# Four small moves on VectorE and its port in an attention plus two-MLP kernel: decoding units on ScalarE, one-input forms, the port in the plan, half the planning cushion

## Chip, core and metric

The kernel runs on one core of a Trainium2 chip. The metric is device time in microseconds (us), of which the median over several runs is compared. The engines are named as in the profile: PE is the matrix engine (PEld its weight loads), DVE is VectorE, ACT is ScalarE, POOL is GpSimd, SP is the queue that issues most of the DMAs.

## What is computed

Causal attention with a decay bias, then a SoLU MLP with a norm, then a second MLP, on 4 batches of 576 tokens (2304 rows) with 8 heads of 64:

```
scores = q @ k.T / 8, masked causally, + min(bias, 0)
bias   = -(cum[row] - cum[col]),  cum = cumsum(max(s, 0))
attn   = exp(scores - rowmax) / (rowsum + 1e-9);   x = attn @ v
h  = x @ w_in (512 x 1024);  e = softmax(h);  y = h * e
ln = (y - mean(y)) / sqrt(var(y) + 1e-6) * g_ln;   x2 = ln @ w_out (1024 x 512)
h2 = x2 @ w2_in (512 x 2048);  g = h2 * clip(h2 + 3, 0, 6) / 6;  out = g @ w2_out (2048 x 512)
```

The weights of the MLPs come as 64-bit floats, so each has to be decoded on the chip. Every matrix that enters a product is split into a high and a low part in the matmul's reduced 32-bit format, and a product is three matmuls (high by high, high by low, low by high).

## The kernel before

**Order.** Nothing is ordered by hand. Every operation is put on a list (`plan.add`) with its engine, a planned duration, the things that it reads and writes and the buffers that it takes. `Plan.emit` then plays the list through: at each step the engine that can start first takes the ready operation of the lowest rank, its planned duration is added, and the order in which the operations start in this play is the order in which they are written out. On the chip every engine runs its own queue in that order. The durations thus set only the order, and never a time on the chip. Two more things enter the play: an operation with `port=True` (all of POOL's unless told otherwise, and some of DVE's) starts only once the last one with the port has ended, and `plan.spare`, set when the first attention round has been listed, adds a cushion to each later operation of an engine.

**Stages.** Four attention rounds, one for each batch, then what is left of the first MLP, then the second. In round one the heads go in pairs: scores on PE, then `tops` (DVE: adds the mask, takes the row minimum of the negated scores, frees the PSUM bank), `both` (DVE: joins the minima of a row cut in two), `exp` (ACT), `inv` (DVE: reciprocal of the row sum) and `go` (POOL: scales the rows), then transposes on PE, copies out of PSUM on DVE and ACT, and the product with V. Beside it run the decoding of the first MLP's weights and its first tiles. In the rounds behind it PE works on the scores of one batch and the first MLP's tiles of the batch before, with an early part of the second MLP's weights in the background.

**Decoding.** `split64` takes 512 columns of 64-bit words for each of 128 rows: a load (`raw_wi` for `w_in`, `raw_wo` for `w_out`, 8 blocks each, issued from ACT's queue), `high` on ACT (the upper word, L369), `units` on DVE (three bits of the lower word, made an integer 0 to 7, L373, tile `t_wi` or `t_wo`), `join` on DVE (shift and or, L377, tile `a_wi` or `a_wo`), `put_hi` (ACT, or DVE for the first four blocks, L384), and `put_lo` (POOL for `w_in`, L393; DVE for `w_out`, L391). The tiles `a` and `t` have one buffer each, so that a block's `high` waits until the block before has gone through `put_lo`, and its `units` until the `join` before has read `t`. The second MLP's weights go through `decoded` in the same way, with its own `units` on DVE.

Of the kernel before, what the change touches and what calls it, by code (L numbers as in the profile page):

```python
# [10 lines left out]
F32 = mybir.dt.float32  # L11
F32R = mybir.dt.float32r
I32 = mybir.dt.int32
U32 = mybir.dt.uint32
BF16 = mybir.dt.bfloat16
AF = mybir.ActivationFunctionType
ALU = mybir.AluOpType
# [22 lines left out]
HI_IN = 4  # L40
# [139 lines left out]
def dve2(n):  # L180
    return 0.11 + 0.00053 * n
# [15 lines left out]
def kernel(ctx, tc, q, k, v, s, w_in, w_out, g_ln, w2_in, w2_out, out):  # L197
    nc = tc.nc
# [4 lines left out]
    P = 128  # L203
# [9 lines left out]
    NQ = len(SZ)  # L213
# [4 lines left out]
    const = ctx.enter_context(tc.tile_pool(name="const", bufs=1))  # L218
# [3 lines left out]
    sums = const.tile([P, NH, NQ], F32, name="sums")  # L222
    rsum = const.tile([P, NH, NQ], F32, name="rsum")
    nmax = const.tile([P, NH, NQ + 1], F32, name="nmax")
    halfs = const.tile([P, 1], F32, name="halfs")
# [21 lines left out]
    def w_out_at(x, c):  # L247
        late = c >= KFF - LATE_OUT
        return w_out_t[x, late][:, c - (KFF - LATE_OUT) * late, :]
# [95 lines left out]

    def split64(plan, pool, src, hi, lo, name, key, scale=None, bufs=1, ring="", raws64=2, after=(), hi_dve=False, on_dve=(), on_pool=(), behind=None, needs=(), home=()):

# [23 lines left out]
        def units():  # L371
            T["t"] = pool_at().tile([P, n], I32, tag="dec_e", name=f"t_{name}", bufs=bufs)
            (nc.gpsimd if "units" in on_pool else nc.vector).tensor_scalar(T["t"], T["raw"][:, :, 0].bitcast(U32), 2.0**-29, 7.0, ALU.mult, ALU.min)  # L373

# [13 lines left out]
        def put_lo():  # L388
# [10 lines left out]
            lambda: plan.add("ACT", 0.61, high, reads=[w], writes=[a], new=[("dec_a" + ring, bufs, a)]),  # L399
            lambda: plan.add(*(("POOL", 0.85) if "units" in on_pool else ("DVE", 0.6)), units, reads=[w], writes=[t], new=[("dec_e" + ring, bufs, t)]),  # L400
            lambda: plan.add("DVE", 0.64, join, reads=[t], writes=[a]),
            lambda: plan.add(*(("DVE", 0.42) if hi_dve else ("ACT", 0.62 if scale is None else 0.71)), put_hi, reads=[a, *home], writes=[f"{key}/h{name}"]),
            lambda: plan.add(*(("DVE", 0.72) if scale is not None or "low" in on_dve else ("POOL", 1.4)), put_lo, reads=[a, f"{key}/h{name}"], writes=[f"{key}/l{name}"]),
        ]
# [10 lines left out]
    def decoded(pool_at, x, k, tags, ready):  # L415
# [6 lines left out]
        def block(o):  # L422
# [22 lines left out]
            for f in (  # L445
                lambda: plan.add("SP", 1.5, load, reads=[ready] if ready else [], writes=[raw], new=[(raw_tag, 1, raw)], lag=2.0),
                lambda: plan.add("ACT", 0.61, high, reads=[raw], writes=[f"{a_key}/{o}"], new=[(a_tag, 1, a_key)] if o == 0 else []),
                lambda: plan.add("DVE", 0.45, units, reads=[raw], writes=[t], new=[(t_tag, 1, t)]),
                lambda: plan.add("DVE", 0.65, join, reads=[t], writes=[f"{a_key}/{o}"], port=True),
            ):  # L450
                f()
# [68 lines left out]
    def load_w_in(c):  # L520
        f = slice((c // KDM) * 512, (c // KDM) * 512 + 512)
        c %= KDM
        done.append([f"win/hwi{c}_{f.start // 512}"])
        return split64(plan, dec, w_in[c * P : (c + 1) * P, f], w_in_h[:, c, f], w_in_l[:, c, f], f"wi{c}_{f.start // 512}", "win", after=["HL0k/h0"], behind=done[-3], hi_dve=c + f.start // 128 < HI_IN)

    def load_w_out(c):
        late = c >= KFF - LATE_OUT
        key = "wlate" if late else "wout"
        done.append([f"{key}/hwo{c}"])
        first = [lambda: plan.add("ACT", 0.0, lambda: w_out_part(True), writes=["wlate/"], new=[("wlate", 1, "wlate")])] if c == KFF - LATE_OUT else []  # L530
        return first + split64(plan, dec, w_out[c * P : (c + 1) * P, :], lambda: w_out_at("h", c), lambda: w_out_at("l", c), f"wo{c}", key, g_sb[:, c : c + 1], behind=done[-3])

# [194 lines left out]
    def exps(h, t, pieces):  # L727
        n, w = SZ[t], ST[t] + SZ[t]

        def both():  # L730
            nc.vector.tensor_tensor(nmax[:n, h, t : t + 1], nmax[:n, h, t : t + 1], nmax[:n, h, NQ : NQ + 1], ALU.min)

# [103 lines left out]
    def norm_part(heads, part):  # L836
# [4 lines left out]
        def inv():  # L841
            r = rsum[:, h0 : h1 + 1, ts[0] : ts[-1] + 1]
            nc.vector.tensor_scalar_add(r, sums[:, h0 : h1 + 1, ts[0] : ts[-1] + 1], 1.0e-9)
            nc.vector.reciprocal(r, r)
# [138 lines left out]
    def ffn1_x(i):  # L983
# [18 lines left out]
        x_keys = [f"x{b}/{hp}_{a}" for _, n, b, o in spans for hp in range(NPAIR) for a in range(2) if (o < CUT if a == 0 else o + n > CUT)]  # L1002
        plan.add("DVE", dve2(512), high, reads=x_keys, writes=[f"xs{i}/h"], new=[("xs", 2, f"xs{i}")])
        plan.add("POOL", pool_tt(512), low, reads=x_keys + [f"xs{i}/h"], writes=[f"xs{i}/l"])
# [15 lines left out]
    def ffn1_stats(i):  # L1020
# [6 lines left out]
        def both():  # L1027
            nc.vector.tensor_tensor(st(2), st(0), st(1), ALU.min)

# [164 lines left out]
    for b, share in enumerate(SHARES):  # L1194
        main = []
        if b == 0:
# [5 lines left out]
            mix(main, mixed([x[:2] for x in first_tiles], early[len(early) // 4 :]))  # L1202
            plan.spare = {"DVE": 0.06, "ACT": 0.1, "POOL": 0}
            continue
# [441 lines left out]
```

## Time and profile before

| | |
|---|---|
| three runs | 806.32, 810.79, 811.64 us, median 810.79 |
| the profiled execution | 803.45 us, of which its span is 801.6 us |
| PE busy | 769.8 us, 96% of the span |
| DVE busy | 606.9 us, 76% |
| ACT busy | 470.9 us, 59% |
| POOL busy | 230.1 us, 29% |

Busy time is the time in which an engine has at least one instruction of its own under way. An instruction that has been taken up and waits for something inside the engine counts as busy. The chain is the work that ended last, followed back from the end of the span to what released each step. All times of the trace are counted from the start of the span.

### The profile page before, as it was taken

To read this page: it belongs to the slowest core of one execution; us is meant where nothing else is said; L and a number is where in the kernel's file an instruction comes from. 1 tells how busy PE (TensorE), PEld (TensorE's weight loads), DVE (VectorE), ACT (ScalarE), POOL (GpSimd) and SP (SyncE) were. 2 spreads that over 40 slices of the span, in tenths; PEclk is the share of its full clock that TensorE was granted. 3 is DMA by queue.
4 is the path that set the end of the run, shared out by engine and by line. 5 is a ranking of instruction groups with operands and counts; after the bars stand their busy time and mean duration, and the time that the engine had idled before them with its cause. 6 is when DMAs were issued, how large, how long until landed. Compare 5 with 4: busy or idle time off the path is not lost.

```text
span 801.6 us, 15887 instructions
## 1 busy us (share of the span) xinstructions
PE 769.8 (96%) x5560; PEld 705.3 (88%) x5560; DVE 606.9 (76%) x1389; ACT 470.9 (59%) x1055; POOL 230.1 (29%) x320
## 2 busy tenths in 40 slices
PE   6779999999999999999999999999997999999998
PEld 5556777988897989888999999999997999999997
DVE  6989977877867688645879898988886876666662
ACT  4758867856765667655474766666674444444441
POOL 3566454334631636343300000000122002222221
PEclk9989999999999999999999999999999999999999
DMA  9947478868668857614151755667499654444440
GB/s 211 209 117 204 112 198 195 211 188 221 147 169 203 230 138 190 181 28 145 37 188 56 246 168 172 203 204 261 142 292 372 214 142 129 129 130 132 132 130 27
DMA packets 157616, 136.34 MB, mean 170 GB/s; under 512 B 67616, under 2 KB 135200, under 8 KB 157536
## 3 DMA queue, kind: packets, MB, share of 16 engines
q1 hardware_dynamic: 153600, 122.07, 54.4%
q10 hardware_dynamic: 2400, 8.54, 3.3%
q0 software_dynamic: 1536, 4.72, 1.6%
q8 instruction: 44, 0.72, 0.4%
q14 instruction: 36, 0.29, 0.1%
HBM read 74.67 MB, written 39.39 MB: 142 GB/s over the span
## 4 chain that ended last, share of the span: by engine, by line
PE 85%; DVE 7%; DMA 4%; ACT 1%; issue 1%; POOL 1%; SPq 0%; DVEq 0%; ACTq 0%
PE bank L1531 22%; PE bank L1354 21%; PE bank L1104 12%; PE bank L1014 11%; PE bank L909 6%; PE bank L814 5%; PE bank L882 5%; PE bank L1083 2%; DVE y L723 1%; PE bank L663 1%; DMA stage<-wt_d 1%; DVE t_wi L373 1%; PE bank L778 1%; POOL y L848 1%; DMA s_sb<-in_s_dram 1%
## 5 line engine op out<-in xcount | busy, mean ns | idle before, releaser
L1354 PE MATMUL bank<-xb,ws 128*128 128x384 f32 x1008 | 176.9, 335 | 3.7 <-ACT c L1367 3.4
L1354 PEld LDWEIGHTS bank<-xb,ws 128*128 128x128 f32 x1008 | 174.4, 188 | 4.7 <-ACT c L1367 4.1
L1531 PE MATMUL bank<-W,fs 128*128 128x256 f32 x864 | 106.8, 283 | 0.3 <-ACT c L1540 0.3
L1531 PEld LDWEIGHTS bank<-W,fs 128*128 128x128 f32 x864 | 105.0, 192 | 0.5 <-ACT c L1540 0.5
L830 POOL TENSOR_SCALAR y<-y,rsum 128x128 f32<-128x128 f32 (+4 forms) x120 | 72.1, 619 | 96.6 <-DVE rsum L826 59.2
L723 DVE CUSTOM_DVE_ANT_0 y<-bank,mask 96x288 f32<-96x288 f32 (+4 forms) x168 | 74.1, 465 | 26.8 <-PE bank L814 23.6
L735 ACT ACTIVATE y<-y,nmax 128x128 f32<-128x128 f32 (+4 forms) x140 | 83.4, 597 | 16.4 <-DVE nmax L723 12.9
L1104 PE MATMUL bank<-zh,w_out_h 128*128 128x256 f32 x288 | 83.5, 290 | 0.7 <-DVE zl L1090 0.7
L1531 PE MATMUL bank<-W,fa 128*128 128x256 f32 x648 | 81.5, 283 | 2.4 <-ACT fa L1508 1.9
L1531 PEld LDWEIGHTS bank<-W,fa 128*128 128x128 f32 x648 | 79.4, 192 | 2.8 <-ACT fa L1508 2.1
L1104 PE MATMUL bank<-zl,w_out_h 128*128 128x256 f32 x288 | 81.0, 281 | 0.1
L1104 PE MATMUL bank<-zh,w_out_l 128*128 128x256 f32 x288 | 80.9, 281 | 0.0
L1388 POOL DMA_DIRECT2D g_d<-g x24 | 13.1, 549 | 187.7 <-DVE g L1383 187.7
L814 PE MATMUL bank<-stack 128*96 128x288 f32 (+4 forms) x288 | 58.4, 319 | 3.2 <-DMA stack<-rows_d 1.7
L1014 PE MATMUL bank<-w_in_h,xh 128*128 128x512 f32 x144 | 60.3, 419 | 0.0
L882 PE MATMUL bank<-ident,y 128*128 128x128 f32 (+2 forms) x420 | 52.2, 261 | 6.1 <-DVE nmax L723 3.6
L1104 PEld LDWEIGHTS bank<-zh,w_out_h 128*128 128x128 f32 x288 | 54.2, 188 | 2.9 <-DVE zl L1090 1.1
L1014 PE MATMUL bank<-w_in_h,xl 128*128 128x512 f32 x144 | 56.6, 393 | 0.0
L1014 PE MATMUL bank<-w_in_l,xh 128*128 128x512 f32 x144 | 56.5, 392 | 0.0
L1508 ACT CAST fs<-r 128x1024 fp32r<-128x1024 f32 x27 | 28.3, 1048 | 45.4 <-PE bank L1531 23.6
L1104 PEld LDWEIGHTS bank<-zh,w_out_l 128*128 128x128 f32 x288 | 54.3, 189 | 0.4
L1104 PEld LDWEIGHTS bank<-zl,w_out_h 128*128 128x128 f32 x288 | 54.3, 188 | 0.3 <-DVE zl L1090 0.3
(274 smaller groups left out, 1576.0 us busy)
## 6 DMA issues: line engine op xcount, KB each, us to landing
r<-g_d SPq DMA_DIRECT2D x36, 512.0 KB
g_d<-g SPq DMA_DIRECT2D x72, 192.0 KB
rawo<-in_moe_w_out_dram SPq DMA_DIRECT2D x16, 512.0 KB
rawi<-in_moe_w_in_dram SPq DMA_DIRECT2D x16, 512.0 KB
x_d<-x2s SPq DMA_DIRECT2D x36, 128.0 KB
xr<-x_d SPq DMA_DIRECT2D x6, 768.0 KB
g_d<-g POOLq DMA_DIRECT2D x24, 192.0 KB, 5.4
W<-wp_d SPq DMA_DIRECT2D x6, 768.0 KB
```

The lines of the kernel that those rows point to most:

```text
L723: nc.vector.tensor_tensor_reduce(out=ys[h, t][:n, c0:c1], in0=bank(key)[:n, : c1 - c0], in1=mask[:n, 480 + n - w + c0 : 480 + n - w + c1], ...
L735: nc.scalar.activation(out=y[:n], in_=y[:n], func=AF.Exp, bias=nmax[:n, h, t : t + 1], scale=-1.0, accum_out=sums[:n, h, t : t + 1])
L814: nc.tensor.matmul(bank(key)[:n, : c1 - c0], lhsT=ss[:, 2 - 2 * m, ST[t] : w], rhs=ss[:, 3 - 2 * m, c0:c1], start=(m == 0), stop=(m == 1))
L830: nc.gpsimd.tensor_scalar(ys[h, t][:n], ys[h, t][:n], rsum[:n, h, t : t + 1], 1.0, ALU.mult, ALU.mult)
L882: nc.tensor.transpose(bank(key)[: SZ[jj], c : c + SZ[t]], ys[h, t][: SZ[t], ST[jj] : ST[jj] + SZ[jj]], ident[: SZ[t], : SZ[t]])
L909: nc.tensor.matmul(bank(key)[j * D : (j + 1) * D, lo - c0 : c1 - c0], lhsT=vs[v_key(p, a)][:n, jj, j, :], rhs=pts[pt_key(2 * p + j, a)][:n ...
L1014: nc.tensor.matmul(bank(key), lhsT=xs[i][m // 2][:, kk, :], rhs=(w_in_l if m == 1 else w_in_h)[:, kk, f * 512 : (f + 1) * 512], start=(kk ...
L1083: nc.tensor.transpose(bank(key)[:, m * P : (m + 1) * P], es[i][:, f, m * P : (m + 1) * P], ident)
L1104: nc.tensor.matmul(bank(key)[:, : 2 * P], lhsT=w_out_at(w, kk)[:, m * P : (m + 1) * P], rhs=z[:, kk, :], start=(kk == 0 and i == 0), stop= ...
L1354: nc.tensor.matmul(bank(key)[:, :W], lhsT=T[f"ws{k}"][:, WS_OF[op], a, kc * P : (kc + 1) * P], rhs=x_form(bi, op)[:, b, kc, :], start=(fir ...
L1508: nc.scalar.copy(T[name][:, 0], T[key(src)])
L1531: nc.tensor.matmul(bank(b_key)[:, : 2 * P], lhsT=T[name][:, y, k, :], rhs=T[f"W{i}_{q}"][:, k - k0, w, :], start=first and k == 0 and y == ...
```

## The change

- `units` of `split64` (16 calls) goes from DVE to ACT: one activation (copy with a scale of 0.936 times 2 to the minus 29), with the rounding to an integer as before and no minimum, since 0.936 keeps the result below 7.5.
- `both` of the attention and of the first MLP, a minimum of two one-column tiles, becomes a `tensor_scalar` whose second operand is a per-partition scalar: one tensor input in place of two.
- `inv` in `norm_part`, the form used for round one's heads, gets an accumulator output that nobody reads. (`norm`, used for most of the other rounds' heads, is not touched.)
- In the list, `port=True` is given to `join`, to `put_lo` on either engine, to `units` of `decoded` and to the `high` of the first MLP's input tiles. Some planned durations are adjusted.
- The cushion behind round one is halved: DVE 0.06 to 0.03, ACT 0.1 to 0.05.

```diff
+    rsum_all = const.tile([P, 1], F32, name="rsum_all")
...
         def units():
             T["t"] = pool_at().tile([P, n], I32, tag="dec_e", name=f"t_{name}", bufs=bufs)
-            (nc.gpsimd if "units" in on_pool else nc.vector).tensor_scalar(T["t"], T["raw"][:, :, 0].bitcast(U32), 2.0**-29, 7.0, ALU.mult, ALU.min)
+            if "units" in on_act:
+                nc.scalar.activation(out=T["t"], in_=T["raw"][:, :, 0].bitcast(U32), func=AF.Copy, scale=0.936 * 2.0**-29)
+            else:
+                nc.vector.tensor_scalar(T["t"], T["raw"][:, :, 0].bitcast(U32), 2.0**-29, 7.0, ALU.mult, ALU.min)
...
-            lambda: plan.add(*(("POOL", 0.85) if "units" in on_pool else ("DVE", 0.6)), units, reads=[w], writes=[t], new=[("dec_e" + ring, bufs, t)]),
-            lambda: plan.add("DVE", 0.64, join, reads=[t], writes=[a]),
+            lambda: plan.add(*(("ACT", 0.61) if "units" in on_act else ("DVE", 0.5)), units, reads=[w], writes=[t], port=not ("units" in on_act), new=[("dec_e" + ring, bufs, t)]),
+            lambda: plan.add("DVE", 0.68, join, reads=[t], writes=[a], port=True),
...
-            lambda: plan.add(*(("DVE", 0.72) if scale is not None or "low" in on_dve else ("POOL", 1.4)), put_lo, reads=[a, f"{key}/h{name}"], writes=[f"{key}/l{name}"]),
+            lambda: plan.add(*(("DVE", 0.72) if scale is not None or "low" in on_dve else ("POOL", 1.4)), put_lo, reads=[a, f"{key}/h{name}"], writes=[f"{key}/l{name}"], port=True),
...
-                lambda: plan.add("DVE", 0.45, units, reads=[raw], writes=[t], new=[(t_tag, 1, t)]),
+                lambda: plan.add("DVE", 0.45, units, reads=[raw], writes=[t], new=[(t_tag, 1, t)], port=True),
...
-            nc.vector.tensor_tensor(nmax[:n, h, t : t + 1], nmax[:n, h, t : t + 1], nmax[:n, h, NQ : NQ + 1], ALU.min)
+            nc.vector.tensor_scalar(nmax[:n, h, t : t + 1], nmax[:n, h, t : t + 1], nmax[:n, h, NQ : NQ + 1], None, ALU.min)
...
-            nc.vector.tensor_scalar_add(r, sums[:, h0 : h1 + 1, ts[0] : ts[-1] + 1], 1.0e-9)
+            nc.vector.tensor_scalar(r, sums[:, h0 : h1 + 1, ts[0] : ts[-1] + 1], 1.0e-9, 0.0, ALU.add, ALU.add, accum_out=rsum_all)
...
-        plan.add("DVE", dve2(512), high, reads=x_keys, writes=[f"xs{i}/h"], new=[("xs", 2, f"xs{i}")])
+        plan.add("DVE", dve2(512), high, reads=x_keys, writes=[f"xs{i}/h"], new=[("xs", 2, f"xs{i}")], port=True)
...
-            nc.vector.tensor_tensor(st(2), st(0), st(1), ALU.min)
+            nc.vector.tensor_scalar(st(2), st(0), st(1), None, ALU.min)
...
-            plan.spare = {"DVE": 0.06, "ACT": 0.1, "POOL": 0}
+            plan.spare = {"DVE": 0.03, "ACT": 0.05, "POOL": 0}
```

## Rows read from the trace of the kernel before

**Rows 1.** The page, part 1 (engines) and part 4 (the chain, by engine).

```profile
PE 769.8 (96%) x5560; PEld 705.3 (88%) x5560; DVE 606.9 (76%) x1389; ACT 470.9 (59%) x1055; POOL 230.1 (29%) x320
...
PE 85%; DVE 7%; DMA 4%; ACT 1%; issue 1%; POOL 1%; SPq 0%; DVEq 0%; ACTq 0%
```

**Rows 2.** Busy time by stretch: length, engines, PE clock, DMA share, GB/s.

```profile
24.00:38.00 14.00, 10.03 (x92) 7.30 (x90) 13.76 (x50) 10.42 (x33) 7.45 (x12) 1.00 0.83 209
38.00:45.00 7.00, 5.24 (x46) 3.39 (x44) 6.34 (x21) 6.59 (x18) 5.16 (x7) 1.00 0.81 167
45.00:50.00 5.00, 1.25 (x11) 1.04 (x11) 5.00 (x4) 1.29 (x4) 4.36 (x5) 0.70 0.47 150
...
60.00:76.00 16.00, 15.96 (x116) 11.12 (x118) 15.45 (x44) 12.96 (x31) 9.00 (x11) 1.00 0.76 208
...
170.00:200.00 30.00, 30.00 (x216) 24.25 (x215) 25.84 (x76) 20.13 (x56) 14.99 (x21) 1.00 0.84 209
```

**Rows 3.** The chain in order of time: start, length, what.

```profile
25.81 0.48 DVE t_wi L373
...
29.74 1.19 DVE rsum L843
...
35.20 1.34 DVE t_wi L373
...
44.97 4.67 DVE t_wi L373
...
50.06 2.08 PE bank L882 x11
52.14 2.06 PE bank L909 x8
...
60.51 1.15 DVE t_wo L373
...
72.89 0.24 DVE t_wo L373
...
80.69 1.80 PE bank L882 x18
...
112.00 0.80 PE bank L909 x8
```

**Rows 4.** The timeline, 44.9 to 50.1 us: start, length, instruction, idle before.

```profile
44.89 4.75 DVE L373 TENSOR_SCALAR t_wi<-raw_wi 128x512 int32<-128x512 uint32 x1
...
48.31 1.05 POOL L695 MEMSET stack<- 128x1152 f32 x1
...
50.06 2.08 PE L882 MATMUL bank<-ident,y 96*128 96x96 f32 x11 [3.57 <-DVE nmax L723]
```

**Rows 5.** Groups by line and shape, then durations (min/median/max ns) by line.

```profile
L373 DVE TENSOR_SCALAR t_wi<-raw_wi 128x512 int32<-128x512 uint32 x8 | 9.2, 1144 | 0.3 <-DMA raw_wi<-in_moe_w_in_dram 0.3
L373 DVE TENSOR_SCALAR t_wo<-raw_wo 128x512 int32<-128x512 uint32 x8 | 4.4, 553 | 0.0
L731 DVE TENSOR_TENSOR nmax<-nmax 96x1 f32<-96x1 f32 x32 | 7.3, 234 | 0.6
L723 DVE DVE_READ_ACCUMULATOR2_ANT nmax<- 128x1 f32 x96 | 7.8, 81 | 0.0
...
L373 DVE TENSOR_SCALAR t_wi<-raw_wi x8: 412/490/4749, 16.2 to 53.4; 128x512 int32<-128x512 uint32 x8
L843 DVE TENSOR_SCALAR rsum<-sums x8: 154/172/1265, 16.6 to 82.2; 128x4 f32<-128x4 f32 x4, 128x6 f32<-128x6 f32 x4
L1039 DVE TENSOR_SCALAR st<-st x18: 200/214/219, 71.0 to 415.6; 128x1 f32<-128x1 f32 x18
L369 ACT ACTIVATE a_wi<-raw_wi x8: 662/670/702, 17.2 to 55.8; 128x512 f32<-128x512 f32 x8
```

**Rows 6.** Groups of the second MLP by line: busy, mean ns, idle before.

```profile
L1373 DVE TENSOR_TENSOR c<-c,bank 128x384 f32<-128x384 f32 x72 | 38.8, 551 | 15.9 <-PE bank L1354 10.1 <-ACT c L1367 5.5 <-ACT ai L435 0.2
L1367 ACT COPY c<-bank 128x384 f32<-128x384 f32 x72 | 34.3, 480 | 33.7 <-PE bank L1354 31.1 <-DVE g L1383 2.0
```

More of the change, by code (lines that the diff above doesn't have):

```diff
@@ L344, in background, with split64 @@
         return [lambda f=f: later(f) for f in fs]
-    def split64(plan, pool, src, hi, lo, name, key, scale=None, bufs=1, ring="", raws64=2, after=(), hi_dve=False, on_dve=(), on_pool=(), behind=None, needs=(), home=()):
+    def split64(plan, pool, src, hi, lo, name, key, scale=None, bufs=1, ring="", raws64=2, after=(), hi_dve=False, on_dve=(), on_act=(), behind=None, needs=(), home=()):
         n = 512
@@ L523, in load_w_in @@
         done.append([f"win/hwi{c}_{f.start // 512}"])
-        return split64(plan, dec, w_in[c * P : (c + 1) * P, f], w_in_h[:, c, f], w_in_l[:, c, f], f"wi{c}_{f.start // 512}", "win", after=["HL0k/h0"], behind=done[-3], hi_dve=c + f.start // 128 < HI_IN)
+        return split64(plan, dec, w_in[c * P : (c + 1) * P, f], w_in_h[:, c, f], w_in_l[:, c, f], f"wi{c}_{f.start // 512}", "win", after=["HL0k/h0"], behind=done[-3], hi_dve=c + f.start // 128 < HI_IN, on_act=("units",))
     def load_w_out(c):
@@ L530, in load_w_out @@
         first = [lambda: plan.add("ACT", 0.0, lambda: w_out_part(True), writes=["wlate/"], new=[("wlate", 1, "wlate")])] if c == KFF - LATE_OUT else []
-        return first + split64(plan, dec, w_out[c * P : (c + 1) * P, :], lambda: w_out_at("h", c), lambda: w_out_at("l", c), f"wo{c}", key, g_sb[:, c : c + 1], behind=done[-3])
+        return first + split64(plan, dec, w_out[c * P : (c + 1) * P, :], lambda: w_out_at("h", c), lambda: w_out_at("l", c), f"wo{c}", key, g_sb[:, c : c + 1], behind=done[-3], on_act=("units",))
     W_IN = {(c, f): [f"win/{x}wi{c}_{f}" for x in "hl"] for c in range(KDM) for f in range(2)}
```

## The prediction

> **What bounds the kernel now.** I read the page's shares and its chain first, to see whose time the end is made of: PE is busy for 96% of the span and is 85% of the chain, DVE is 7% of it [rows 1]. A saving on DVE therefore counts only where DVE is the late one. The table of busy time by stretch says where that is. In round one, from 24 to about 100 us, DVE is full (13.76 of 14 us, 5.00 of 5, 15.45 of 16) while PE has room up to 50 us; in a stretch of the later rounds PE is busy for all 30 of 30 us with DVE at 25.84 [rows 2]. So the change can earn its time in round one, and in the rounds behind it has little to earn and something to lose. Then the chain in order of time, between 24 and 101 us: the reader is to see that many of its pieces are DVE calls that stand in the diff, and that equal calls differ by ten times [rows 3]. The timeline around the longest tells why. One `units` call took 4.75 us, from 44.89 to 49.64 us, and it ended 0.28 us after a POOL memset from 48.31 to 49.36, the last of a run of POOL instructions without a gap [rows 4]. The shortest took 0.41 us; the seven others of `w_in` took 4.5 together (9.2 less 4.7), so 1.6 more than seven of the shortest, and `w_out`'s eight 4.4 [rows 5]. I read this as a DVE call that can't start beside a running POOL instruction and finds no gap.
>
> **Units to ACT: the long stall.** What the 4.67 us on the chain cost PE is read from PE. It was idle for 3.57 us before 50.06 [rows 4], its granted clock is 0.70 in that stretch [rows 2], a mean between the two levels, 1.2 and 2.4 GHz, and the next groups ran slowly: 11 transposes in 2.08 us where 18 take 1.80 later, 8 matmuls in 2.06 where 8 take 0.80 [rows 3]. At the later rates these are 1.10 and 0.80 us, so 0.98 and 1.26 us went to the slow clock. The site costs 3.57 + 0.98 + 1.26 = 5.8 us. With `units` on ACT the DVE queue goes straight on to the `tops` that frees the bank. What is late next is the pair of copies out of PSUM behind the transposes and the low part of the first MLP's input on POOL, so I take 4.5 of the 5.8. The bounds are 5.8, and 0 if another DVE call meets the same POOL run.
>
> **Units to ACT: the other fifteen.** DVE loses 13.6 us in all (9.2 + 4.4) [rows 5], 9.0 without the long one. Between 24 and 38 us three of them stand on the chain, 0.48 and 1.34 and one of 0.35 between, 2.17 us [rows 3]. ACT gets the calls. No row shows this activation; the nearest is `high`, which reads the same strided words on the same 512 columns in 0.67 us [rows 5]; I take 0.67 us each, with 0.5 and 0.75 as bounds, 10.7 us for 16. Here the cover is thin: ACT is at 10.42 of 14 us in that stretch and at 6.59 of 7 in the next [rows 2]. Three calls more in the first make 12.4 us of work, and if the stretch shrank by 2.17 it would be 11.8 us long. ACT would take DVE's place, so I count 0.8 us of 2.17 (from minus 1 to 2.2). Between 60 and 76 us three more, the first 1.15 and the last 0.24 with one of 0.35 between, are 1.74 us of chain [rows 3], but PE is busy for 15.96 of 16 there with matmuls of the first MLP [rows 2]; I count 0.8 (0 to 1.7). Elsewhere I count nothing. Behind a `units` on ACT are queued the next exponentials, the copies out of PSUM and the next weight load, which ACT issues. `units` waits for the `join` before it (one buffer of `t`), which is over sooner than the `put_lo` for which `high` waits already, so it adds no wait of its own; `join` on DVE now waits about 0.6 us longer for ACT, and DVE's next calls with it if the list has them that close.
>
> **One-input forms.** `inv` of round one: 8 calls with a median of 172 ns and a longest of 1265 [rows 5]; one stands on the chain with 1.19 us [rows 3]. The accumulator output adds a read of about 0.08 us per call [rows 5]. If the new form isn't held, the site gives 1.19 - 0.17 - 0.08 = 0.94 us; it lies in the stretch where ACT fills up, so I count 0.4 (minus 0.1 to 0.9). `both`: 32 calls took 7.3 us, 234 ns on the average [rows 5]. The nearest row to the new form is L1039, a `tensor_scalar` with a per-partition scalar on one column, median 214 ns and never over 219 [rows 5]. 32 times 0.02 us is 0.6 us less on DVE; the 18 calls of the first MLP change likewise, where PE is full. I count 0.2 us, between minus 0.5 and 1.
>
> **The port in the list.** This costs nothing on the chip; it moves the places of calls in the order. It lets the play see a DVE call wait behind POOL, which is what the chip did. I have no row that prices an order, and count 0, plus or minus 2 us.
>
> **Half the cushion.** Planned against measured: a 384-column DVE call is 0.484 us and with its cushion 0.544 before, 0.514 after, and took 0.551; an ACT copy is 0.416, 0.516 before, 0.466 after, and took 0.480 [rows 6] (lengths that overlap a little from call to call). With the old cushion the play was about right or slow, with the new one it is a bit fast: PE's products will be placed before their inputs are there. An excess of cushion cost nothing that I can see in the later rounds, since PE is full there [rows 2]. So I count a loss of 1.0 us, between a gain of 1 and the rival below.
>
> **Sum.** 4.5 + 0.8 + 0.8 + 0.4 + 0.2 - 1.0 = 5.7 us, against the profiled execution of 803.45 us (801.6 of span and 1.85 around it). PE is full behind round one, so a saving there reaches the end. That execution lay below all three timed runs, which spread over 5.3 us; taken off their median, 810.79 - 5.7 = 805.1 us. About 1%, 8 us, is what I take a measurement of this kernel to tell from no change.
>
> **Rivals.**
>
> 1. All that DVE is relieved of comes back: 13.6 us of `units`, and a PE that is no longer slowed. DVE's full stretches speak for it [rows 2], ACT's load up to 45 us against it. Five of the sixteen calls stand outside 24 to 101 us; at 0.41 each they are taken off, which leaves 11.5 us; with 0.9 for `inv` and 0.6 for `both` that is 13.0, and 797.8 us. Chance 0.24.
> 2. The stall only moves. POOL's run up to 49.4 us is still there, and `join`, the casts of the tiles and the reciprocals stay on DVE. The first of them that falls into it is held as `units` was. Then 4.5 is lost from the sum: 1.2 us, 809.6 us. Against it: the seven other `units` of `w_in`, no less exposed, were held for 1.6 us all together [rows 5]. Chance 0.17. The Trainium skill, "SBUF — State Buffer", section "Who interferes with whom", says that a DVE call with two SBUF inputs contends only with a GpSimd instruction that reads SBUF. By that rule a `join` in this place would be free at the memset, at 48.31, a us sooner; no row here shows it.
> 3. Slower: PE waits at the head of its queue in rounds two to four. Rounds two to four hold 24 heads in some 220 us, so 9 us a head, in which DVE and ACT have about 23 and 17 calls by the 76 and 56 of a 30 us stretch [rows 2]; the halved cushion moves the play by 23 times 0.03 = 0.7 us on DVE and 17 times 0.05 = 0.85 on ACT. It decides as soon as DVE's and ACT's lead on PE is smaller than that: 0.8 us for each of 24 heads is 19 us, less 6.7 gained in round one, 823 us; at half of the heads 814. For it: DVE at 25.84 of 30 leaves little to catch up with. Against it: eight banks and two buffers of each score tile in between. Chance 0.12.
> 4. ACT becomes round one's bound. Between 24 and 45 us it is busy for 17.0 of 21 us [rows 2], and five calls of 0.67 make 20.4. If they stand ahead of the exponentials and copies for which PE waits, 3.4 us come back late: 4.5 + 0.2 - 1.0 - 3.4 = 0.3 us, 810.5 us. Against it: they have rank 50 places behind. Chance 0.08. The trace says that a call with 0.41 us of work on DVE, unhindered, takes 0.67 on ACT [rows 5]. The Trainium skill, "ScalarE: Activation LUTs", section "Rules for kernel authors", speaks against the move in the same way: multiplications and minima belong on VectorE, which is faster for them. By that rule alone 16 times 0.26, 4 us of engine time, would be added.
>
> **The numbers.** Forecast 0.39, rivals 0.24, 0.17, 0.12 and 0.08. The likeliest is 805.1 us with 801 to 808 as its own range. The range goes from 797.5 (the first rival) to 814.5 (the third at half of the heads). Faster by over 1% (below 802.7): the first rival and a third of the forecast's lower half, 0.35. Slower by over 1% (above 818.9): most of the third rival, 0.11. Within: 0.54.
>
> **What would show it.** Right: no DVE call of over 2 us in round one, L373 under ACT with some 0.67 us each and ACT above 90% between 24 and 45 us, the granted clock at 1.00 between 45 and 60, the first `norm` of round two some 5 us earlier, and the same distance at the end. Wrong: a new long DVE call beside a POOL run, PE idle time in 140 to 400 us, or a different wait where the second MLP's weights come in at 600 us.

## The result and the profile after

The changed kernel took 799.25 us (median of five runs, 795.95 to 803.99) against 810.79 us for the kernel before on the same chip (five runs, 806.32 to 811.78). The ratio is 0.9882, with an interval of 0.9848 to 0.9916: 9.6 us less by the ratio, 11.5 by the medians. The forecast was 805.1 us, the first rival 797.8.

The profiled execution of the changed kernel took 798.7 us, of which 796.9 is its span, so the two traces differ by only 4.75 us. The trace of the kernel before is from the low end of its times (803.45 us; 35 runs of that kernel in a later comparison went from 802.62 to 818.02, median 808.62). What follows from two traces can therefore place half of the gain at the most.

Lines of `kernel.py` stand one to four further down in the changed kernel: `units` is L375 (L373 before), `join` L381, `both` L735, round one's `inv` L847, `tops` L727, transposes L886, products with V L913, first scores L782, the first MLP's first product L1018.

The page of the changed kernel, part 1 (engines) and part 4 (the chain, by engine):

```profile
PE 771.1 (97%) x5560; PEld 707.0 (89%) x5560; DVE 595.1 (75%) x1381; ACT 478.2 (60%) x1071; POOL 228.3 (29%) x320
...
PE 80%; DMA 7%; DVE 6%; ACT 3%; issue 2%; POOL 1%; SPq 1%; DVEq 0%; ACTq 0%; POOLq 0%
```

DVE lost 11.8 us of busy time and ACT gained 7.3 [rows 1]. PE's share of the chain went down from 85 to 80%, and DMA's up from 4 to 7%. The calls themselves came out as expected. Groups of the changed kernel by line and shape:

```profile
L375 ACT ACTIVATE t_wi<-raw_wi 128x512 int32<-128x512 uint32 x8 | 5.4, 673 | 1.0 <-DMA raw_wi<-in_moe_w_in_dram 1.0
L375 ACT ACTIVATE t_wo<-raw_wo 128x512 int32<-128x512 uint32 x8 | 5.3, 665 | 0.0
```

and durations (min/median/max ns) by line:

```profile
L735 DVE TENSOR_SCALAR nmax<-nmax x32: 170/208/211, 29.0 to 345.9; 96x1 f32<-96x1 f32 x32
L847 DVE TENSOR_SCALAR_CACHE_REDUCE rsum<-sums x8: 148/154/160, 16.3 to 84.9; 128x4 f32<-128x4 f32 x4, 128x6 f32<-128x6 f32 x4
L847 DVE DVE_READ_ACCUMULATOR rsum<-sums x8: 82/83/84, 16.4 to 85.0; 128x1 f32 x8
```

`units` takes 0.67 us on ACT, as taken from `high`; `both` and `inv` are not held in this trace (211 and 160 ns at the longest; `inv` reached 1265 before [rows 5]). But the place that was to pay for it all did not. Busy time by stretch, first of the changed kernel, then of the kernel before for two stretches that the rows ahead of the prediction don't hold:

```profile
24.00:38.00 14.00, 10.27 (x89) 7.24 (x87) 10.67 (x44) 12.52 (x37) 7.64 (x13) 0.91 0.95 225
38.00:45.00 7.00, 6.45 (x38) 4.18 (x36) 2.98 (x12) 5.96 (x16) 2.23 (x2) 0.70 0.62 156
45.00:50.00 5.00, 2.22 (x20) 1.36 (x18) 4.77 (x17) 4.27 (x11) 5.00 (x6) 0.90 0.74 188
...
60.00:101.00 41.00, 41.00 (x319) 30.56 (x316) 34.82 (x112) 34.83 (x83) 21.30 (x32) 1.00 0.63 161
101.00:140.00 39.00, 38.35 (x293) 32.98 (x292) 32.95 (x105) 30.75 (x81) 17.98 (x32) 1.00 0.80 203
```

```profile
60.00:101.00 41.00, 39.74 (x295) 29.94 (x296) 39.57 (x119) 33.09 (x81) 23.70 (x32) 1.00 0.61 160
101.00:140.00 39.00, 36.82 (x266) 29.15 (x265) 30.26 (x95) 26.62 (x70) 19.16 (x30) 1.00 0.79 193
```

Up to 50 us DVE is relieved (10.67 of 14 us, 2.98 of 7), and PE is no better for it: the granted clock falls to 0.91 and then 0.70, where it was 1.00 before up to 45 us [rows 2], and from 45 to 50 us POOL is busy throughout and PE for 2.22 us. Behind 60 us PE is full in both kernels or nearly so, but in the same 80 us it gets through 612 matmuls instead of 561. The chain of the changed kernel shows the new hold-up (start, length, what):

```profile
29.87 6.20 DMA raw_wi<-in_moe_w_in_dram
...
36.15 0.66 ACT t_wi L375
36.81 0.55 ACT a_wi L370
37.36 0.37 ACT pt5a L890
37.78 1.54 PE bank L913 x5
...
44.04 2.09 POOL y L852 x2
...
48.80 1.38 POOL y L852 x2
50.23 4.05 PE bank L886 x22
```

The timeline of the changed kernel at its two ends:

```profile
33.71 0.69 PE L667 MATMUL bank<-ident,rawk 96*128 96x96 f32 x6 [1.78 <-DMA rawk<-in_k_dram]
...
34.76 0.48 ACT L890 COPY pt4a<-bank 128x384 f32<-128x384 f32 x1
...
36.15 0.66 ACT L375 ACTIVATE t_wi<-raw_wi 128x512 int32<-128x512 uint32 x1 [0.20 <-DMA raw_wi<-in_moe_w_in_dram]
37.27 0.46 ACT L890 COPY pt5a<-bank 128x384 f32<-128x384 f32 x1
37.78 0.69 PE L913 MATMUL bank<-pt5a,V2a 128*64 128x256 f32 x1 [1.41 <-ACT pt5a L890]
...
44.04 3.52 POOL L852 TENSOR_SCALAR y<-y,rsum 128x384 f32<-128x384 f32 x3 [3.01 <-PE bank L782]
...
50.23 1.17 PE L886 MATMUL bank<-ident,y 96*128 96x96 f32 x5 [2.29 <-POOL y L852]
```

and the same two copies on ACT in the kernel before:

```profile
34.34 0.45 ACT L886 COPY pt4a<-bank 128x384 f32<-128x384 f32 x1
34.70 0.47 ACT L886 COPY pt5a<-bank 128x384 f32<-128x384 f32 x1
```

A weight load was issued at 29.87 us and landed at 36.07. `units` stands ahead of `high` and of a copy out of PSUM in ACT's queue; the copy `pt5a` came 1.1 us after `units` had started, and PE sat idle for 1.41 us. Most of that is not a wait for the load: ACT was busy with exponentials until 0.20 us before `units` started, and idle for 1.0 us in all ahead of the eight `units` of `w_in`. It is the time of `units` and `high` themselves, which now stand, with one exponential, between the two copies: `pt5a` starts 2.5 us behind `pt4a`, before it was 0.4. Nor is it the whole of the loss. PE had been idle for 1.78 us up to 33.71, waiting for a load of k, and the granted clock was at its lower level (0.50, 1.2 GHz) from 35.4 to 42.2 us, so it fell ahead of this `units`. Waits of that kind, for a load of q or k around 32 us, stand in the traces of units_only, all_but_port, all_but_forms and load_late below as well (1.70, 2.54, 1.84 and 1.73 us) and not in the trace of before; no run tests it, and why the load is late is not shown. The scores that follow are late, POOL begins its run of row scalings at 44.04 us, and the transposes wait for it until 50.23, with PE idle for 2.3 us and at the lower clock behind it (0.50 from 49.1 to 55.8 us). DVE hardly comes into it. From 54 to 101 us the chain is PE alone, where before it had pieces of DVE [rows 3].

To put a number on it I worked out, for each stretch, what PE lost: the length of the stretch less the matmuls in it, each at what its line takes back to back at the full clock (0.2325 us for L1018, 0.0900 for L886, 0.1075 for L913, and so on). One execution of each kernel stands behind a row, and executions of one kernel differ by several us, so only differences of some us are read.

| PE lost, us | 16 to 45 | 45 to 60 | 60 to 101 | 101 to 140 | 140 to 245 | behind 245 |
|---|---|---|---|---|---|---|
| before | 10.1 | 6.3 | 5.1 | 5.4 | 4.9 | 9.9 |
| after | 11.7 | 6.3 | 3.2 | 1.5 | 3.9 | 10.2 |
| units_free (below) | 9.6 | 1.5 | 8.0 | 6.9 | 3.0 | 10.7 |
| load_late (below) | 9.9 | 0.7 | 6.6 | 4.4 | 11.0 | 9.5 |

The changed kernel loses as much at the long stall's place as before, 1.6 us more ahead of it, and 5.8 us less between 60 and 140 us.

### The profile page after: what moved, and what is told of

It reads as the page before. It is cut to its first block, busy times and chain, and to the rows that moved or that the text cites. A ratio compares the mean times of both kernels' runs of the same rounds, so it can differ in the third digit from the quotient of the medians.

```text
span 796.9 us, 15897 instructions
## 1 busy us (share of the span) xinstructions
PE 771.1 (97%) x5560; PEld 707.0 (89%) x5560; DVE 595.1 (75%) x1381; ACT 478.2 (60%) x1071; POOL 228.3 (29%) x320
## 4 chain that ended last, share of the span: by engine, by line
PE 80%; DMA 7%; DVE 6%; ACT 3%; issue 2%; POOL 1%; SPq 1%; DVEq 0%; ACTq 0%; POOLq 0%
PE bank L1535 23%; PE bank L1358 18%; PE bank L1108 10%; PE bank L1018 8%; PE bank L913 6%; PE bank L886 5%; PE bank L818 5%; PE bank L782 2%; DMA stage<-wt_d 2%; DMA rawo<-in_moe_w_out_dram 2%; DMA xr<-x_d 2%; PE bank L1087 1%; PE bank L667 1%; DMA rawi<-in_moe_w_in_dram 1%; DMA raw_wi<-in_moe_w_in_dram 1%
## 5 line engine op out<-in xcount | busy, mean ns | idle before, releaser
L834 POOL TENSOR_SCALAR y<-y,rsum 128x128 f32<-128x128 f32 (+4 forms) x120 | 72.5, 623 | 98.2 <-DVE rsum L830 84.9
L727 DVE CUSTOM_DVE_ANT_0 y<-bank,mask 96x288 f32<-96x288 f32 (+4 forms) x168 | 74.2, 466 | 26.2 <-PE bank L818 21.4
L1018 PE MATMUL bank<-w_in_h,xh 128*128 128x512 f32 x144 | 60.2, 418 | 0.0
L1018 PE MATMUL bank<-w_in_h,xl 128*128 128x512 f32 x144 | 56.6, 393 | 0.0
L1018 PE MATMUL bank<-w_in_l,xh 128*128 128x512 f32 x144 | 56.4, 392 | 0.0
L886 PE MATMUL bank<-ident,y 128*128 128x128 f32 (+2 forms) x420 | 52.3, 265 | 2.3 <-POOL y L852 2.3
```

Source lines behind the costliest of these rows:

```text
L727: nc.vector.tensor_tensor_reduce(out=ys[h, t][:n, c0:c1], in0=bank(key)[:n, : c1 - c0], in1=mask[:n, 480 + n - w + c0 : 480 + n - w + c1], ...
L834: nc.gpsimd.tensor_scalar(ys[h, t][:n], ys[h, t][:n], rsum[:n, h, t : t + 1], 1.0, ALU.mult, ALU.mult)
L886: nc.tensor.transpose(bank(key)[: SZ[jj], c : c + SZ[t]], ys[h, t][: SZ[t], ST[jj] : ST[jj] + SZ[jj]], ident[: SZ[t], : SZ[t]])
L1018: nc.tensor.matmul(bank(key), lhsT=xs[i][m // 2][:, kk, :], rhs=(w_in_l if m == 1 else w_in_h)[:, kk, f * 512 : (f + 1) * 512], start=(kk ...
```

## The experiments

Each ran in five rounds beside the kernel before on the same chip. The ratio is to that kernel, with its 95% interval.

### One part alone

**units_only**: the kernel before with the 16 `units` on ACT, planned at 0.61.

```diff
-            (nc.gpsimd if "units" in on_pool else nc.vector).tensor_scalar(T["t"], T["raw"][:, :, 0].bitcast(U32), 2.0**-29, 7.0, ALU.mult, ALU.min)
+            nc.scalar.activation(out=T["t"], in_=T["raw"][:, :, 0].bitcast(U32), func=AF.Copy, scale=0.936 * 2.0**-29)
...
```

> Only the 16 units calls go to ACT. If the relief of DVE in round one makes the gain, this alone is 5 to 9 us below the kernel before (ratio 0.989 to 0.994), with DVE under 90% busy between 60 and 101 us. If the order (port in the list, cushion) makes it, this is within 2 us of the kernel before, or above it where ACT waits for a weight load at the head of its queue.

Measured: 807.03 us, ratio 0.9986 (0.9960 to 1.0013). The main part, by itself, is not told from no change. By the count above PE loses about 5.6 us between 45 and 60 us in this kernel's trace, 4.4 between 60 and 101 and 5.8 between 101 and 140: no `units` is held on DVE any more, and yet the stall's place costs nearly what it did.

**forms_only**: `both` and `inv` in their new forms, nothing else; every engine's instructions stand in the order of the kernel before.

```diff
-            nc.vector.tensor_tensor(nmax[:n, h, t : t + 1], nmax[:n, h, t : t + 1], nmax[:n, h, NQ : NQ + 1], ALU.min)
+            nc.vector.tensor_scalar(nmax[:n, h, t : t + 1], nmax[:n, h, t : t + 1], nmax[:n, h, NQ : NQ + 1], None, ALU.min)
...
-            nc.vector.tensor_scalar_add(r, sums[:, h0 : h1 + 1, ts[0] : ts[-1] + 1], 1.0e-9)
+            nc.vector.tensor_scalar(r, sums[:, h0 : h1 + 1, ts[0] : ts[-1] + 1], 1.0e-9, 0.0, ALU.add, ALU.add, accum_out=rsum_all)
...
```

> Only both and inv in their new forms; planned durations are untouched, so every queue has the order of the kernel before, and what changes is the chip's alone. My sum has 0.6 us for them (0.4 and 0.2): ratio 0.998 to 1.001. If held small calls were the cost of round one, 2 to 3 us less (ratio below 0.997), since inv is no longer held for 1.2 us twice.

Measured: 807.57 us, ratio 0.9986 (0.9959 to 1.0012). No effect that can be told.

**port_only**: the port in the list and the planned durations, `units` left on DVE.

```diff
...
-            lambda: plan.add("DVE", 0.64, join, reads=[t], writes=[a]),
+            lambda: plan.add("DVE", 0.68, join, reads=[t], writes=[a], port=True),
...
```

> Only the port flags and the planned durations that belong to them; no instruction changes, only the order. My sum has 0 plus or minus 2 us (ratio 0.9975 to 1.0025). If the order makes the gain, 4 us or more below the kernel before, with fewer DVE calls held for over 1 us in round one.

Measured: 810.79 us, ratio 1.0023 (0.9995 to 1.0052). In the new order the long `units` is gone (1.06 us at most), but three other calls of the decoding are held, and PE waits for the `tops` behind them. The timeline of this kernel on DVE, then its chain where that ends:

```profile
59.56 1.33 DVE L377 SCALAR_TENSOR_TENSOR a_wo<-a_wo,t_wo 128x512 int32<-128x512 int32 x1
60.93 0.97 DVE L373 TENSOR_SCALAR t_wo<-raw_wo 128x512 int32<-128x512 uint32 x1
61.82 1.74 DVE L391 SCALAR_TENSOR_TENSOR w_out_l<-a_wo,g_sb,w_out_h 128x512 fp32r<-128x512 f32 x1
```

```profile
64.36 0.36 DVE y L723
...
64.78 1.02 PE bank L882 x4
```

PE was idle for 3.64 us ahead of the last line. By the count above PE loses 2.5 us between 45 and 60 us in this kernel and 11.2 between 60 and 101. So telling the play of the port moved the stall and did not remove it.

**cushion_only**: half the cushion.

```diff
-            plan.spare = {"DVE": 0.06, "ACT": 0.1, "POOL": 0}
+            plan.spare = {"DVE": 0.03, "ACT": 0.05, "POOL": 0}
```

> Only the cushion behind round one is halved; round one is the same instruction for instruction, only the order behind it changes. My sum has a loss of 1.0 us (between a gain of 1 and a loss of 12). If a smaller cushion earns something, PE idle time from 125 us on goes down and the time is 2 us or more below the kernel before.

Measured: 810.00 us, ratio 0.9999 (0.9968 to 1.0030). Nothing, either way.

### All but one part

These are the changed kernel with one part taken back.

**all_but_units**: `units` on DVE again (planned at 0.5, with the port).

```diff
-        return split64(plan, dec, w_in[c * P : (c + 1) * P, f], w_in_h[:, c, f], w_in_l[:, c, f], f"wi{c}_{f.start // 512}", "win", after=["HL0k/h0"], behind=done[-3], hi_dve=c + f.start // 128 < HI_IN, on_act=("units",))
+        return split64(plan, dec, w_in[c * P : (c + 1) * P, f], w_in_h[:, c, f], w_in_l[:, c, f], f"wi{c}_{f.start // 512}", "win", after=["HL0k/h0"], behind=done[-3], hi_dve=c + f.start // 128 < HI_IN)
...
```

> The changed kernel with the 16 units back on DVE (with the port in the list). If the relief of DVE makes the gain, this is back at 805 to 810 us. If the order makes it, within 2 us of the changed kernel's 799.

Measured: 815.55 us, ratio 1.0066 (1.0036 to 1.0096): slower than before. Without the move the rest does harm; the longest `units` of `w_in` is 2.38 us in it.

**all_but_port**: the `port=True` that the change added to DVE's calls taken back.

```diff
...
-            lambda: plan.add("DVE", 0.68, join, reads=[t], writes=[a], port=True),
+            lambda: plan.add("DVE", 0.68, join, reads=[t], writes=[a]),
...
```

> The changed kernel without the port flags on DVE's calls; the same instructions in another order. If the port in the list is worth nothing, within 2 us of 799. If it makes the gain, 803 us or more.

Measured: 802.48 us, ratio 0.9900 (0.9861 to 0.9938).

**all_but_cushion**: the old cushion.

```diff
-            plan.spare = {"DVE": 0.03, "ACT": 0.05, "POOL": 0}
+            plan.spare = {"DVE": 0.06, "ACT": 0.1, "POOL": 0}
```

> The changed kernel with the old cushion; round one is the changed kernel's. By my sum 1 us below 799; if the halved cushion earns something, 801 us or more.

Measured: 801.50 us, ratio 0.9899 (0.9857 to 0.9941).

**all_but_forms**: the old forms of `both` and `inv`; the order is that of the changed kernel on every engine.

```diff
-            nc.vector.tensor_scalar(nmax[:n, h, t : t + 1], nmax[:n, h, t : t + 1], nmax[:n, h, NQ : NQ + 1], None, ALU.min)
+            nc.vector.tensor_tensor(nmax[:n, h, t : t + 1], nmax[:n, h, t : t + 1], nmax[:n, h, NQ : NQ + 1], ALU.min)
...
```

> The changed kernel with both and inv in their old forms; planned durations are untouched, so every queue has the changed kernel's order, and the difference is the chip's alone. If units and the order are the gain, within 2 us of the changed kernel's 799. If the forms are half of it (units alone gave 1.5 us, units with forms and cushion 8), 804 us or more, with inv held for 1 us and more again.

Measured: 799.48 us, ratio 0.9880 (0.9845 to 0.9916), beside the changed kernel's 0.9882. The forms are worth nothing that can be told. With `units` on ACT any one of the three other parts can go, and about 1% stays.

### The hold by itself

Was it the work that left DVE, or the waiting of `units` for POOL inside DVE? **units_free** leaves `units` on DVE, in the place that it had in every queue (the order of all five engines is that of the kernel before), and gives it a form with an accumulator output that nobody reads.

```diff
+    units_all = const.tile([P, 1], F32, name="units_all")
...
-            (nc.gpsimd if "units" in on_pool else nc.vector).tensor_scalar(T["t"], T["raw"][:, :, 0].bitcast(U32), 2.0**-29, 7.0, ALU.mult, ALU.min)
+            nc.vector.tensor_scalar(T["t"], T["raw"][:, :, 0].bitcast(U32), 0.936 * 2.0**-29, 0.0, ALU.mult, ALU.add, accum_out=units_all)
```

> The kernel before with units still on DVE, in a form with an accumulator output, and without the minimum (a scale of 0.936 in its place); the order is the kernel before's. If units was held for the port, the call of 4.75 us becomes one of some 0.65, PE's granted clock stays at 1.00 between 45 and 60 us, and 3 to 5 us are gained, less up to 2 for 16 calls of 0.65 in place of 0.41. If it was something else, the long call is still there. If the wait only moves to the next call or to POOL, the time is within 1 us of the kernel before.

Measured: 800.98 us, ratio 0.9897 (0.9859 to 0.9934). Durations of `units` in this kernel (min/median/max ns), and the timeline of its DVE and POOL around the call that took 4.75 us before:

```profile
L374 DVE TENSOR_SCALAR_CACHE_REDUCE t_wi<-raw_wi x8: 656/676/686, 15.8 to 49.0; 128x512 int32<-128x512 uint32 x8
L374 DVE DVE_READ_ACCUMULATOR t_wi<-raw_wi x8: 77/82/83, 16.4 to 49.6; 128x1 f32 x8
L374 DVE TENSOR_SCALAR_CACHE_REDUCE t_wo<-raw_wo x8: 669/675/686, 54.7 to 119.8; 128x512 int32<-128x512 uint32 x8
```

```profile
42.89 2.16 POOL L849 TENSOR_SCALAR y<-y,rsum 96x576 f32<-96x576 f32 x2
44.67 0.67 DVE L374 TENSOR_SCALAR_CACHE_REDUCE t_wi<-raw_wi 128x512 int32<-128x512 uint32 x1
45.02 1.28 POOL L394 TENSOR_TENSOR w_in_l<-a_wi,w_in_h 128x512 fp32r<-128x512 f32 x1
46.27 1.28 POOL L1001 TENSOR_TENSOR xl<-x,xh 128x512 fp32r<-128x512 f32 x1
47.49 1.05 POOL L696 MEMSET stack<- 128x1152 f32 x1
```

```profile
45.00:60.00 15.00, 14.84 (x105) 10.74 (x103) 13.13 (x37) 10.17 (x24) 12.29 (x13) 1.00 0.64 185
60.00:101.00 41.00, 36.56 (x271) 27.54 (x268) 36.94 (x119) 30.91 (x77) 21.43 (x30) 1.00 0.62 160
```

POOL's run is still there without a gap, from 42.89 to 48.54 us, and the call starts in the middle of it and is through in 0.67 us. All sixteen take 0.66 to 0.69 us. Before, sixteen unhindered calls would have been 6.6 us (16 times 0.412), and 7.0 of the 13.6 us were waiting [rows 5]; here 12.1 us (16 times 0.676 and 0.08 for the read) are all work. So DVE's work in `units` grew by 5.5 us, only the waiting left it, and the gain is that of the changed kernel within the intervals. In this order, then, the hold counted and the load did not. POOL's own work is not what got shorter: it is busy for 230.0 us here and 230.1 before [rows 1]. That the changed kernel's gain is the same hold is not shown by this. The Trainium skill, "SBUF — State Buffer", section "Who interferes with whom", says that `tensor_scalar` can take the port pair shared with GpSimd, though not in the form that also writes out its accumulator. The trace agrees: 656 to 686 ns in this form, 412 to 4749 in the other [rows 5].

The windows above, the last fence, are of this kernel: between 45 and 60 us the clock is 1.00 and PE loses 1.5 us in place of 6.3. Behind it, 60 to 140 us, it loses 4.4 more than the trace of before. The gain thus stands elsewhere than the changed kernel's, for nearly the same time; and the spans of the two traces differ by 2.6 us (801.6 and 799.0), so they can't say where the rest of the 9 us lies.

**free_forms**: units_free with the new forms of `both` and `inv`, again in the order of the kernel before.

```diff
+            nc.vector.tensor_scalar(T["t"], T["raw"][:, :, 0].bitcast(U32), 0.936 * 2.0**-29, 0.0, ALU.mult, ALU.add, accum_out=units_all)
...
+            nc.vector.tensor_scalar(nmax[:n, h, t : t + 1], nmax[:n, h, t : t + 1], nmax[:n, h, NQ : NQ + 1], None, ALU.min)
...
```

> The kernel before, in its own order, with units on DVE in the accumulator form and both and inv in the new forms: no call of the diff can be held for the port, and DVE has all its work and more. If the holding is what counted, 8 to 11 us below the kernel before, as low as the changed kernel or lower. If DVE's load counts too, it stays above the changed kernel by 2 us or more.

Measured: 800.90 us, ratio 0.9903 (0.9868 to 0.9939), beside 0.9897 without them. After forms_only and all_but_forms this is the third pair of equal orders in which the forms are worth nothing that can be told.

**all_free**: the changed kernel with `units` on DVE in the accumulator form, planned at 0.65 and without the port.

```diff
...
+                nc.vector.tensor_scalar(T["t"], T["raw"][:, :, 0].bitcast(U32), 0.936 * 2.0**-29, 0.0, ALU.mult, ALU.add, accum_out=units_all)
...
+            lambda: plan.add(*(("ACT", 0.61) if "units" in on_act else ("DVE", 0.65)), units, reads=[w], writes=[t], port=False, new=[("dec_e" + ring, bufs, t)]),
...
```

> The changed kernel (forms, port in the list, halved cushion) with units on DVE in the accumulator form, planned at 0.65 us and without the port. If ACT's relief is worth something beside the free form, below the changed kernel by 2 to 4 us. If the order that the port flags give to round one with units on DVE is bad in itself (815 us in the kernel with held units), 805 us or more.

Measured: 811.43 us, ratio 1.0035 (1.0000 to 1.0070). No `units` is held here either (686 ns at most), and all of the gain is gone: with the port list and the planned durations the order is another one, and PE loses 8.1 us between 101 and 140 and 10.2 between 245 and 360 us, where the changed kernel loses 1.5 and 4.4. An order can take back as much as the hold is worth.

### The new wait

**load_late**: the changed kernel with the weight load's planned lag at 6.5 us in place of 4.0, which is nearer to the 6.20 us of the chain, so that the play puts `units` and `high` later in ACT's queue.

```diff
-                             lag=2.0 if behind is None else 4.0, after=after),
+                             lag=2.0 if behind is None else 6.5, after=after),
```

> The changed kernel with the weight loads planned to land 6.5 us after their issue in place of 4.0, as the one on the chain did (6.2). If units wait for a load at the head of ACT's queue and hold the copies behind them, and that costs the 6 us that PE loses between 45 and 60 us, 2 to 5 us below the changed kernel. If not, within 2 us of it, or above, since the first MLP's weights come later.

Measured: 801.93 us, ratio 0.9914 (0.9881 to 0.9948). The stretches of this kernel:

```profile
45.00:60.00 15.00, 14.86 (x109) 11.18 (x108) 11.28 (x37) 10.97 (x26) 12.15 (x13) 1.00 0.65 179
...
140.00:245.00 105.00, 100.17 (x744) 86.39 (x743) 74.51 (x235) 66.40 (x177) 43.94 (x71) 0.98 0.73 185
```

and its chain in the second of them:

```profile
152.35 3.92 DMA rawk<-in_k_dram
156.27 0.67 ACT ao L439
156.94 0.48 ACT zh L1090
157.45 0.70 DVE zl L1094
158.20 2.18 PE bank L1108 x10
```

with ACT's timeline at the start of it:

```profile
156.26 0.68 ACT L439 ACTIVATE ao<-rawo 128x512 f32<-128x512 f32 x1 [6.04 <-DMA rawk<-in_k_dram]
```

With the later places PE loses 0.7 us between 45 and 60 us and 1.8 less ahead of it, and the first normalisation of round two starts at 92.1 in place of 97.6 us. So the loss there belongs to the order and not to `units` being on ACT as such. Which instruction's place it was is not shown: the longer lag moves instructions on every engine from about 20 us on. And of these 7.4 us nothing is left: between 60 and 245 us PE loses 22.0 us in place of 8.6, in an execution of 804.32 us, 2.4 above this kernel's median. The largest piece is in the chain above. ACT stood idle for 6.04 us at the head of its queue, ahead of the `high` of a block of the second MLP (L439). The profile puts that wait down to a load of k, but this call reads `rawo`, a weight load. The casts of the inputs of the first MLP's second product stand behind it, first on ACT and then on DVE, and PE was idle for 3.81 us.

No kernel here was faster than the changed one. units_free is as good within the intervals, with one call's form changed.

## Why the prediction was right and wrong

The sign and the range held; the time, 799.25 us, lies below the forecast's own range of 801 to 808 and next to the first rival. By the ratio, 9.6 us off 810.79, it is 801.2 us, at the lower end of that range. That the sum came so near is in part luck: its largest term was not won where it was counted, and something else made up for it. By the steps:

- **The long stall, 4.5 us.** This is the step that failed. That `units` was held beside POOL's run, and that this cost PE 4 to 6 us, was right: with the hold alone taken away, PE loses 4.8 us less between 45 and 60 us. That the move to ACT would win it was wrong: PE loses 6.3 us there in both kernels and 1.6 more ahead of it. I had said that `units` on ACT "adds no wait of its own" because its buffer comes free early. The wait did stay small (0.20 us for the load at the place on the chain, 1.0 us over eight calls). What this term put at nothing is what the calls' own time costs those behind them: I had named the exponentials and copies queued there, and only rival 4 gave them a price; `pt5a` starts at 37.27 us in place of 34.70, with POOL's scalings late behind it. The idle time before 33.71 us, for a load of k, I did not foresee at all; how the loss divides between the two stays open.
- **The other fifteen, 1.6 us.** Under-sized, if it is theirs. Between 60 and 140 us PE loses 5.8 us less than before. I had counted 0.8 in one part of it, from the calls that stood on the chain, and nothing elsewhere, since PE was busy for 15.96 of 16 us. A busy PE was not a PE at its peak: before, between 60 and 101 us, it lost 5.1 us by the count while it was idle for 1.26. The chain before ran through DVE there, and DVE was at 39.57 of 41 us; it is at 34.82 now. That I should have priced, not PE's busy share. But only 1.9 of the 5.8 us lie in that stretch. The other 3.9 lie between 101 and 140 us, where DVE is busier than before (32.95 us against 30.26), and units_only, with the same move, loses about as much as the kernel before in both stretches. So the move alone does not bring the 5.8 us, and what else it takes is not shown.
- **The forms, 0.6 us.** The new durations were right (0.208 us against 0.214 expected, the read of 0.08), and there is no hold in the calls that were changed. The price of the old `both` was misread: 234 ns is a mean with held calls in it, and the middle call took 155 (the line below, from the trace of before), so the new form is 0.05 us longer where nothing holds it. The 32 calls went from 7.3 to 6.2 us all the same, because the held ones are gone. What the forms are worth can't be told from nothing: 0.9986 (0.9959 to 1.0012) alone, and no difference in the two other pairs of equal orders, which 0.6 us fits.

```profile
L731 DVE TENSOR_TENSOR nmax<-nmax x32: 144/155/835, 37.2 to 352.9; 96x1 f32<-96x1 f32 x32
```

- **The port in the list, 0 plus or minus 2.** With `units` on ACT it holds (0.9900 without it, 0.9882 with it). With `units` on DVE it was too narrow: the order it makes is up to 0.66% slower, together with the other parts.
- **Half the cushion, minus 1.0.** Not borne out: 0.9999 alone, and 0.9899 without it beside 0.9882 with it.
- **Rival 1** had the time (797.8), not the reason: it credits all work that leaves DVE, and units_free leaves 12.1 of 13.6 us on DVE for the same gain. **Rival 2** had half of the reason: the stall did move, though not to another DVE call, and the time (809.6) was wrong because the gain came from elsewhere. **Rival 3** fell: PE loses 8.3 us between 140 and 360 us, 10.1 before. **Rival 4** saw that ACT would stand in PE's way in round one. ACT reaches 18.48 of 21 us between 24 and 45, 88%, and where PE waits for ACT in this trace it is the place of `units` and `high` in the queue that makes the copy late. The rival's time, 810.5, was wrong for the same reason as the second's.
- **What would show it.** No DVE call over 2 us in round one: so (1.36 at most). ACT above 90% between 24 and 45: 88. Clock at 1.00 between 45 and 60: 0.77, no. The first normalisation 5 us earlier: 97.6 in place of 98.2, no. The last score product, though, starts at 345.2 in place of 353.5 and the second MLP at 409.3 in place of 415.0.
- **Two sums.** The chance of 0.35 for below 802.7 us is more than its parts make: 0.24 and a third of half of 0.39 are 0.31. The range's upper end of 814.5 stands for the third rival at half of the heads, which is 814 by its own terms.

**What stays open.** units_only takes the hold away too, and gains 0.14% with an upper end at 0.4, and its trace loses about 5.6 us at the stall's place, as the changed kernel's does; with half the cushion or the port list beside it (all_but_port, all_but_cushion) the same move gains 1.0%. Neither part does anything alone. All four orders differ from each other, and all_free, port_only and load_late show that an order can give back 5 to 10 us at another place; that this is the reason here is argued, not shown. So the move of `units` is needed for the changed kernel's gain (all_but_units has none) and is not enough for it, and what makes up that gain is not shown. Where in the execution the 9 us of units_free lie is open as well.

## What to carry to other kernels

When equal calls on one engine have very different durations, try a form of the call that can't be held before moving it to another engine: here one line kept the order and brought as much as the whole change. In another order the same form brought nothing (all_free), so it has to be measured in its place. Before a call goes to another engine, read what it waits for, and price its own time for what stands behind it in the new queue. Where a planner makes the order from planned times, take parts back one at a time: alone, each part measured 0.14% or less to the good, and together 1.2%.

## What the hardware showed that was not expected

- The accumulator output makes the call longer and steadier: `units` takes 0.676 us where the plain form takes 0.412 at the shortest, and its longest is 0.686 against 4.749. The added read is 0.08 us and overlaps its neighbours.
- A hold doesn't last until POOL has a gap, as I had read it [rows 4]. Round one of cushion_only issues the same instructions in the same order as before, and the same call took 1.46 us from 47.19, ending 0.3 us after one POOL instruction gave way to the next without a gap; in the trace of before it let three such changes pass and took 4.75 us. The timeline of cushion_only, then durations in it and in forms_only (min/median/max ns):

```profile
47.04 1.32 POOL L393 TENSOR_TENSOR w_in_l<-a_wi,w_in_h 128x512 fp32r<-128x512 f32 x1 [0.20 <-ACT w_in_h L386]
47.19 1.46 DVE L373 TENSOR_SCALAR t_wi<-raw_wi 128x512 int32<-128x512 uint32 x1
48.32 1.45 POOL L1000 TENSOR_TENSOR xl<-x,xh 128x512 fp32r<-128x512 f32 x1
```

```profile
L373 DVE TENSOR_SCALAR t_wi<-raw_wi x8: 385/422/1456, 16.5 to 52.3; 128x512 int32<-128x512 uint32 x8
```

```profile
L374 DVE TENSOR_SCALAR t_wi<-raw_wi x8: 388/502/4751, 16.1 to 52.2; 128x512 int32<-128x512 uint32 x8
```

  So whether the long hold happens differs from one execution or order to the next, and a sum that takes it from one trace takes a chance. That cushion_only, with a short hold in its trace, was no faster over its runs warns of the same.
- ACT reads 32-bit integers and writes rounded ones at the price of a plain copy: 0.646 to 0.692 us in the changed kernel's 16 calls of 512 strided words, where `high`, without a conversion, takes 0.662 to 0.702 [rows 5].
